# Block 6's first product by seven half-size products, with the opening's figures, the tail's stores and delays of output products

## The chip, the cores and the metric

The kernel runs on one core of a Trainium2 chip. The core has five engines with a queue each: TensorE (PE in the profile, with its weight loads as PEld), VectorE (DVE), ScalarE (ACT), GpSimd (POOL) and SyncE (SP, which here only issues transfers). They wait for one another by semaphores. PE writes to PSUM alone, eight banks of 128 partitions by 512 floats; DVE and ACT read PSUM and write to SBUF or back to PSUM. The metric is device microseconds of one execution. The time before is a median of 287.68 us over three runs (287.2 to 288.32).

## The reference

```python
scores = scale * np.matmul(q, k.transpose(0, 1, 3, 2))       # 8 batches, 8 heads, 576 positions, 64 wide
gamma = 1.0 - 2.0 ** (-5.0 - np.arange(H, dtype=np.float32))
rel = pos[:, None] - pos[None, :]
Dmat = np.where(rel >= 0, gamma[:, None, None] ** rel[None, :, :], 0.0)
attn_out = np.matmul(scores * Dmat[None, :, :, :], v)
x = np.ascontiguousarray(attn_out.transpose(0, 2, 1, 3)).reshape(B * S, H * D)    # 4608 x 512
h = x @ w_in                                                  # 4608 x 2048
g = 0.5 * h * (1.0 + erf(h / sqrt(2)))
return g @ w_out                                              # 4608 x 512
```

So an attention with a decay per head in place of a softmax comes first, and then a perceptron with a GELU between two products. Inputs and output are float32; inside, matrices are bf16 and sums are float32 in PSUM.

## The kernel before, in words

**Attention.** The 576 positions of a sequence are cut in five chunks, four of 128 and one of 64. A *unit* is one chunk of one batch (the short chunks of two batches make one unit), 36 units in all, mostly in pairs. A unit needs q and k transposed (`turn` on PE for the first groups, `turn_dma` on SP's queue for the rest), scores (`scores`, tile sc), a decay mask on DVE (`masked`, tile ret, two DVE instructions for a unit), values scaled by position (`scaled_v`, tile vh; one DVE instruction, or eight on ACT for units named in `BY_ACT`), output products (`inner`, tile o_ps), a running state of keys and values (`state`, tile u_ps), the part that comes from earlier chunks (`cross`) and the way out of PSUM into xT (`evacuate`). A pair's scores take four PSUM banks, its outputs two.

**The perceptron.** The 4608 rows are nine blocks (0 to 8) of 512, four units each. The first product of blocks 0 to 6 is plain (`mlp1`, line 683, tile hT): 64 matmuls of 512 columns for a block, or the same in smaller cuts for blocks 0 and 1, each group followed by a GELU on ACT (line 692). Blocks 7 and 8, those from `FAST` on, take it by seven half-size products instead of eight (`fast`, line 935, tile f): for each of four column groups j, the products P1 to P7 have four matmuls of 256 columns each. Their operands are sums and differences: of w_in (`sum_in`, lines 893 to 895, and `sum_last`, line 900, which overwrites a quarter of each w_in piece once the last plain block has read it) and of xT (`sum_x`, line 908). What the products give is put together in PSUM and SBUF: P1 and P7 are copied, P6 and P5 are added on DVE (lines 950 and 954), and four GELUs on ACT follow (lines 956 and 960). A group holds up to four PSUM banks.

The second product is plain for block 0 (`mlp2`, line 727, tile oT) and by seven half-size products for blocks 1 to 8 (`part`, line 855, tile m, products M1 to M7, with `after` for what DVE and ACT do behind each). Its operands are sums of g (`sum_g`, lines 757 to 761) and of w_out (`sum_w`). M6 and M7 end with the output tiles `hi` and `lo`, which `store` (line 710) sends out on SP's queue; in the last block M6's are issued from ACT's queue, and M7 comes in two halves.

**What sets the order.** The program is written out by a planner in the kernel's own source, at build time. It keeps a clock for each engine (`T`), with a cost for each operation, models the two DMA queues, and at each step writes out the piece of PE's work that is ready: attention steps first (`cand` and `due`), then perceptron pieces (`mlp_pick`). Where a first product by halves runs beside the second product of the block before, two of its products go to one of the second product (`A_TURNS`). A candidate must find free PSUM banks (`held`, `pending`, `free_time`). Conditions tie the pieces down: `AHEAD` bounds how many units attention runs ahead, `fast_ready` says when a half-size product may start. Until 16 us the planner puts filler matmuls into gaps of PE (`warm`, line 1132), behind eight fixed ones (line 1139); before the time `HOT` it takes matmuls as twice as long.

The list `ORDER` (line 325) is worked off by POOL, which issues all loads of weights (wi, wo) and of q, k and v in that order, and makes a few constants (io, dq). Its entries a... name units whose values ACT scales, and s... give a delay to a unit's scores (`S_LATE`). The first q and k are loaded by SP and ACT.

Of the kernel before, what the change touches and what calls it, by code (L numbers as in the profile page):

```python
# [17 lines left out]
def kernel(  # L18
# [51 lines left out]
    HW_FIRST = ((("q", 0),), (("k", 0),))  # L70
    FAST, ALL_FAST = 7, 7
    N_LD = 5
# [4 lines left out]
    A_TURNS = 2  # L77
    HOT = 7.5

# [240 lines left out]
    for x, keys in enumerate(zip(*HW_FIRST)):  # L320
        for n, (what, i) in enumerate(keys):
            land[what, i] = 4.75 + 1.7 * x
            t = tiles_of(i)
            cast_due[what, i] = (t[1] if what == "v" else t[0][:, "qk".index(what)], first[what, i])
    ORDER = ("wi1 k2 q1 io k1 q2 v0 v1 wi0 v2 k3 wi2 wi3 wi4 q3 wi5 wi6 v3 wi7 v4 k5 k4 q5 q4 wo1 wo0 v5 q8 wo2 "
# [3 lines left out]
             "s20+4.0 s5+3.0 s15+0.3").split()  # L329

    BY_ACT = {int(x[1:]) for x in ORDER if x[0] == "a"}
    S_LATE = {int(x[1:].split("+")[0]): float(x.split("+")[1]) for x in ORDER if x[0] == "s"}
    ORDER = [x for x in ORDER if x[0] not in "as"]

# [372 lines left out]

    def store(t, ts, src, lo=0, hi=d_model, queue=nc.sync):
        for row, p0, n in rows_of(t, ts):
            queue.dma_start(out[row:row + n, lo:hi], src[p0:p0 + n])  # L710
        for _ in rows_of(t, ts):
            hw_dma(0.4, MOVE["store"] * (hi - lo) / d_model / len(rows_of(t, ts)), max(T["act"], T["dve"]), putter(o_free, (t, ts // 2)))
# [78 lines left out]
    def after(t, p, done, half):  # L791
# [12 lines left out]
        elif p == M1:  # L804
            v = held_bank[t, "V", 0] = seeded([128, 2, 256], "m")
            for x in range(1 + last):
                xs = slice(x, x + 1) if last else slice(0, 2)
                at = either(0.42 if last else 0.68, done, v[1][:, xs], held_bank[t, "Z", x][1], -1.0)
        elif p in (M5, M2):
            at = either(0.68, max(done, o_at(t, p == M2)), lo[:, :, RIGHT] if p == M5 else hi[:, :, LEFT], m)  # L810
            release(b, at + SEM)
        elif p == M6:
            nc.vector.scalar_tensor_tensor(hi[:, :, RIGHT], m, -1.0, hi[:, :, LEFT], op0=ALU.mult, op1=MINUS)  # L813
            at = on("dve", 0.68, max(done, read_at[t, M2]))
            release(b, at + SEM)
            for x in range(2):
                if last:
                    store(t, 2 + x, hi[:, x, RIGHT], 256, 512, nc.scalar)
                else:
                    store(t, 2 + x, hi[:, x, :])  # L820
        elif last:
            nc.vector.tensor_tensor(lo[:, half, LEFT], m[:, 0], lo[:, half, RIGHT], op=MINUS)
            at = on("dve", 0.42, done)
            release(b, at + SEM)
            store(t, half, lo[:, half, LEFT], 0, 256)
        else:
            nc.vector.tensor_tensor(lo[:, :, LEFT], m, lo[:, :, RIGHT], op=MINUS)
            at = on("dve", 0.68, max(done, read_at[t, M5]))
            release(b, at + SEM)
            for x in range(2):  # L830
                store(t, x, lo[:, x, :])
# [147 lines left out]
    def fast_ready(t, j, p):  # L979
# [3 lines left out]
        if p == P1:  # L983
            if not may_begin(t, j):
                return 1e9
            if wanted[0] and lead()[0] == "3" and lead()[2] in (M3, M4, M1) or len(held) + 3 + pending() > 7:
                return 1e9
            if t >= ALL_FAST and nA < N_U and lead()[0] == "3":
                return 1e9
            if j == 2 and t < ALL_FAST and (t - 1, M1, 0) not in begun:  # L990
# [94 lines left out]
    def fire():  # L1085
# [24 lines left out]
        while later:  # L1110
            n = next((n for n, x in enumerate(later) if x[0] <= now and T[x[1]] <= now + 0.05
                      and (x[1] == "dve" or x[0] < 5.0 or all(y[3] is not make_args for y in later))), None)
# [24 lines left out]
    for _ in range(8):  # L1137
        b, t = bank([128, 512], FP32, "warm")
        nc.tensor.matmul(t, lhsT=zeros[:, :128], rhs=zeros, start=True, stop=True)  # L1139
        release(b, 0.0)  # L1140
    T["pe"] = 4.9
    while True:
# [26 lines left out]
        if nB < nA:  # L1169
# [4 lines left out]
            if any(("v", i) in cast_due for i in back):  # L1174
                ready = 1e9
            ready = max(ready, free_time(out_banks(back) + first_o))
            hurry = early or nA == N_U or stuck
# [7 lines left out]
        if g and scored < 1e8:  # L1185
            if early or stuck:
                cand(max(scored, free_time(2 * len(g))) if nA - nB <= 2 else 1e9, "S", g, [])
            else:
                late = first and (first[0] in "34" and first[1] + 1 >= FAST)
                free = head is None or late or head[1] == 0 or head[0] == "1" and (head[1] > 1 or head[4] > 0)  # L1190
                free = free or head[0] == "2" and 4 <= head[3] <= 8 or head[0] == "3"
                ahead = 4 * (first[1] - (first[0] == "4")) + AHEAD + 2 * (first[1] > 1) + 3 * bool(late) if first else 99
                if (free and all(st[i]["R"] <= now and st[i].get("V", 1e9) <= now + 0.3 for i in back)
# [3 lines left out]
                    if n + len(held) + pending() <= 8 and T["dve"] <= now + 1.0:  # L1197
                        cand(max(scored, free_time(n) - 0.3), "S", g, back)
                    elif n > 7 and n - 2 * len(g) + len(held) + pending() <= 8:
                        cand(free_time(n - 2 * len(g)) - 0.3, "S", [], back)  # L1200
# [93 lines left out]
```

## Time and profile before

| what | us |
|---|---|
| median of three runs | 287.68 |
| the profiled execution, its own time | 287.26 |
| its span, first to last instruction | 285.5 |
| PE busy, DVE busy, ACT busy | 278.0, 191.3, 151.7 |
| first scores (line 500) | 10.59 |
| first matmul of hT | 13.96 |
| second product of block 5 begins | 190.29 |
| first matmul of f (block 7) | 222.23 |
| last DVE instruction begins | 281.38 |

The page gives the busy time of each engine over the span, then groups of instructions with what ended the idle time before them. Matmuls are pipelined: the length given for one is longer than the distance from its start to the start of the next, so the distance is what a matmul costs. A table of stretches gives each engine's busy time in windows of the span, and the waits tell which engine waited for which. Between the span and the execution's own time lie 1.8 us of launch and end.

### The profile page before, as it was taken

The numbers are of one execution on the slowest core, as the hardware profiler recorded it, in microseconds if no ns is written. First come the engines' busy times: TensorE is split into PE (matmuls) and PEld (weight loads), VectorE is DVE, ScalarE is ACT, GpSimd is POOL, SyncE is SP. The second block draws the span as 40 slices with busy tenths as digits, with TensorE's granted clock in tenths as the row PEclk, the third lists the DMA queues.
The fourth block names the chain that finished last, engine by engine and source line by source line (L and its number), as shares of the span: only waits on it lengthen the run. The fifth ranks groups of instructions, "written<-read, shape, count | busy, mean of one in ns | idle before, by whom it ended". The sixth has DMA issues, their size and how long they took to land.

```text
span 285.5 us, 7980 instructions
## 1 busy us (share of the span) xinstructions
PE 278.0 (97%) x3343; PEld 204.5 (72%) x3364; DVE 191.3 (67%) x396; ACT 151.7 (53%) x339; POOL 113.8 (40%) x143
## 2 busy tenths in 40 slices
PE   7999999999999999999999999999999999999994
PEld 1699676688864588548854786468746888888883
DVE  3751693879658782998289717683598768966912
ACT  5678635565428642893255448852267454565320
POOL 8977977897156546412297454000000000000000
PEclk9999999999999999999999999999999999999999
DMA  9999999999999999999999999990210000400233
GB/s 145 164 189 170 194 183 149 214 169 152 138 162 137 193 133 152 225 125 136 158 136 174 139 152 148 228 86 3 76 73 2 0 2 0 149 0 3 76 110 111
DMA packets 152372, 35.39 MB, mean 124 GB/s; under 512 B 141072, under 2 KB 148240, under 8 KB 152336
## 3 DMA queue, kind: packets, MB, share of 16 engines
q0 software_dynamic: 116832, 18.10, 97.8%
q1 hardware_dynamic: 34160, 16.26, 32.8%
q10 hardware_dynamic: 1344, 0.52, 0.8%
q8 instruction: 26, 0.43, 0.7%
q14 instruction: 10, 0.08, 0.1%
HBM read 36.70 MB, written 9.44 MB: 162 GB/s over the span
## 4 chain that ended last, share of the span: by engine, by line
PE 93%; DVE 4%; issue 1%; ACT 0%
PE hT L683 33%; PE m L855 33%; PE f L935 9%; PE oT L727 5%; PE o_ps L584 3%; PE sc L519 3%; DVE ret L542 2%; PE qk_ps L471 2%; PE warm L1139 2%; PE u_ps L603 1%; PE o_ps L635 1%; PE warm L1132 1%; DVE xT L654 0%; PE sc L500 0%; PE sc L509 0%
## 5 line engine op out<-in xcount | busy, mean ns | idle before, releaser
L683 PE MATMUL hT<-xT,w_in 128*128 128x512 bf16 (+2 forms) x689 | 100.8, 300 | 0.8
L692 ACT ACTIVATE g<-hT 128x512 bf16<-128x512 f32 (+1 forms) x128 | 67.4, 542 | 39.9 <-PE hT L683 38.2
L683 PEld LDWEIGHTS <-w_in 128*128 128x128 bf16 x704 | 57.3, 98 | 37.2
L855 PEld LDWEIGHTS <-gs 128*128 128x128 bf16 x640 | 62.1, 98 | 8.4 <-issue 0.6
L855 PE MATMUL m<-w_sum,gs 128*128 128x256 bf16 x384 | 46.5, 273 | 0.4 <-DVE m L802 0.3
L313 POOL DMA_DIRECT2D v_ld<-in_v_dram x40 | 34.1, 865 | 18.7 <-DMA qk_ld<-in_k_dram 8.3
L542 DVE TENSOR_TENSOR ret<-sc,msk 128x512 bf16<-128x512 f32 x48 | 30.2, 682 | 15.4 <-PE sc L519 15.4
L313 POOL DMA_DIRECT2D qk_ld<-in_q_dram x36 | 30.4, 854 | 22.5 <-DMA v_ld<-in_v_dram 11.8
L313 POOL DMA_DIRECT2D qk_ld<-in_k_dram x36 | 30.3, 847 | 21.6 <-DMA qk_ld<-in_q_dram 17.1
L855 PE MATMUL m<-w_out,gs 128*128 128x256 bf16 x256 | 32.4, 273 | 0.0
L855 PE MATMUL m<-w_sum,g 128*128 128x256 bf16 x256 | 30.7, 273 | 0.0
L855 PEld LDWEIGHTS <-g 128*128 128x128 bf16 x256 | 25.0, 98 | 4.0
L757 DVE TENSOR_TENSOR gs<-g 128x1024 bf16<-128x1024 bf16 x32 | 21.7, 685 | 5.4 <-ACT g L692 5.1
L556 ACT ACTIVATE vh<-v_ld,dv 128x64 bf16<-128x64 bf16 x96 | 24.0, 339 | 0.0
L761 DVE TENSOR_TENSOR gs<-g 128x1024 bf16<-128x1024 bf16 x32 | 21.5, 682 | 0.0
L654 DVE TENSOR_TENSOR xT<-o_ps,dqT 128x512 bf16<-128x512 f32 (+1 forms) x32 | 18.4, 615 | 2.0 <-PE o_ps L635 1.9
L450 ACT COPY o<-m 128x512 f32<-128x512 f32 x14 | 8.2, 584 | 20.7 <-PE m L855 20.7
L813 DVE SCALAR_TENSOR_TENSOR o<-m,o 128x512 f32<-128x512 f32 x8 | 5.5, 690 | 20.1 <-PE m L855 15.7
L450 ACT CAST u_sb<-u_ps 128x512 bf16<-128x512 f32 x15 | 8.8, 585 | 18.2 <-PE u_ps L603 18.2
L960 ACT ACTIVATE g<-f 128x512 bf16<-128x512 f32 x24 | 13.6, 591 | 6.9 <-PE f L935 6.9
L445 DVE COPY qkT<-qk_ps 128x512 bf16<-128x512 bf16 x15 | 5.8, 420 | 16.3 <-PE qk_ps L471 16.3
L559 DVE TENSOR_TENSOR vh<-v_ld,dv 128x512 bf16<-128x512 bf16 x24 | 15.7, 680 | 0.0
(96 smaller groups left out, 307.2 us busy)
## 6 DMA issues: line engine op xcount, KB each, us to landing
out_dram<-o SPq DMA_DIRECT2D x29, 256.0 KB, 5.0
v_ld<-in_v_dram POOLq DMA_DIRECT2D x32, 128.0 KB, 9.4
qk_ld<-in_k_dram POOLq DMA_DIRECT2D x28, 128.0 KB, 8.8
qk_ld<-in_q_dram POOLq DMA_DIRECT2D x28, 128.0 KB, 10.4
w_in<-in_moe_w_in_dram POOLq DMA_DIRECT2D x8, 256.0 KB, 7.2
w_out<-in_moe_w_out_dram POOLq DMA_DIRECT2D x8, 256.0 KB, 7.9
out_dram<-o SPq DMA_DIRECT2D x11, 128.0 KB, 2.4
qk_ld<-in_k_dram POOLq DMA_DIRECT2D x8, 64.0 KB, 9.5
```

The lines of the kernel that those rows point to most:

```text
L313: nc.gpsimd.dma_start(dst, src[2 * bp + jj, :, ci * C:ci * C + n, :].rearrange("h s d -> s h d"))
L450: nc.scalar.copy(dst, src)
L542: nc.vector.tensor_tensor(r, t, by, op=ALU.mult)
L556: nc.scalar.activation(vh[:, h, :], loaded[i][1][:, h, :], AF.Copy, scale=dv[:, h, ci:ci + 1])
L559: nc.vector.tensor_tensor(vh, loaded[i][1], dv[:, :, ci:ci + 1].to_broadcast([128, H, D]), op=ALU.mult)
L654: nc.vector.tensor_tensor(x_of(i)[:, :, n * x:n * x + n], o, dqT[:, :, ci * C:ci * C + n], op=ALU.mult)
L683: nc.tensor.matmul(hT[:, m, :], lhsT=w[:, cc, o:o + 128], rhs=x_tiles[t][:, cc, lo:hi], start=(cc == 0), stop=(cc == N_DM - 1))
L692: nc.scalar.activation(g_of(t, m0 // 2)[:, m0 % 2:m0 % 2 + n, lo:hi], hT, AF.Gelu)
L757: nc.vector.tensor_tensor(s.rearrange("p m a b -> p m (a b)"), g[:, :, 0, :], g[:, :, 1, :], op=ALU.add)
L761: nc.vector.tensor_tensor(s, g[:, :, :, LEFT], g[:, :, :, RIGHT], op=MINUS)
L855: nc.tensor.matmul(m[:, 0 if apart else ts, :], lhsT=a, rhs=w, start=p in begins and mm == 0 and ts == 0, stop=mm == N_DF // 2 - 1, skip_g ...
L935: nc.tensor.matmul(m[:, y, :], lhsT=a[:, c], rhs=d[:, c], start=p in (P1, P7) and y == 0 and c == 0, stop=c == 1, skip_group_check=True)
```

## The change

`FAST` and `ALL_FAST` go from 7 to 6, so block 6 takes its first product by seven half-size products too. The rest is in the planner, in its list and in the tail:

- the list of loads, of units scaled on ACT (19 instead of 12) and of delays of scores is another, and entries b... are new: they delay a unit's output products (`B_LATE`);
- for the opening, `HOT` is 9.5 instead of 7.5, PE's clock stands at 6.33 instead of 4.9 behind the fixed fillers, the first loads land at 4.8 instead of 4.75, and leftover constants may be written when their engine is within 0.25 of PE's clock instead of 0.05;
- the condition that kept a first product by halves from starting while attention is unfinished and the second product leads is taken out;
- attention may run as far ahead beside late second products as elsewhere (`3 * bool(late)` becomes `0 * bool(late)`), and output products may be written without scores beside any second product;
- in the last block, M6's last step on DVE is made in two halves, the second half-tile first, each followed by its stores, which go to ACT's queue, SP's queue and ACT's queue.

```diff
-    FAST, ALL_FAST = 7, 7
+    FAST, ALL_FAST = 6, 6
-    HOT = 7.5
+    HOT = 9.5
...
-            land[what, i] = 4.75 + 1.7 * x
+            land[what, i] = 4.8 + 0.75 * x
...
-    ORDER = ("wi1 k2 q1 io k1 q2 v0 v1 wi0 v2 k3 wi2 wi3 wi4 q3 wi5 wi6 v3 wi7 v4 k5 k4 q5 q4 wo1 wo0 v5 q8 wo2 "
-             "wo3 dq2 wo4 wo7 a30 wo6 q6 dq3 v7 k7 wo5 v6 q7 k6 q11 q9 k10 k8 v12 v11 k9 k12 k11 q10 v10 v8 v9 q12 "
...
+    ORDER = ("k1 wi0 io v0 q1 q2 k2 v1 a35 v2 q3 k3 wi1 wi2 v3 wi3 k4 wi4 q4 wi6 wi5 q5 q6 k5 wo0 wi7 wo1 wo2 v4 "
+             "v5 dq2 wo3 wo5 k6 q8 q9 q11 q7 wo4 k7 k10 v6 wo6 v7 a15 v11 wo7 v8 a8 k11 k8 v9 q10 k9 v12 q12 dq3 "
+             "v10 k12 a7 a28 a31 a11 a32 s17+6.0 s35+1.0 s0+0.3 s29+1.5 dq4 s24+0.3 b21+2.0 a27 s8+0.3 s27+6.0 "
...
+    B_LATE = {int(x[1:].split("+")[0]): float(x.split("+")[1]) for x in ORDER if x[0] == "b"}
...
-    def store(t, ts, src, lo=0, hi=d_model, queue=nc.sync):
-        for row, p0, n in rows_of(t, ts):
+    def store(t, ts, src, lo=0, hi=d_model, *on_queues):
+        for x, (row, p0, n) in enumerate(rows_of(t, ts)):
+            queue = on_queues[x] if on_queues else nc.sync
...
-            nc.vector.scalar_tensor_tensor(hi[:, :, RIGHT], m, -1.0, hi[:, :, LEFT], op0=ALU.mult, op1=MINUS)
-            at = on("dve", 0.68, max(done, read_at[t, M2]))
+            for x in (1, 0) if last else (slice(0, 2),):
+                nc.vector.scalar_tensor_tensor(hi[:, x, RIGHT], m[:, x], -1.0, hi[:, x, LEFT], op0=ALU.mult, op1=MINUS)
+                at = on("dve", 0.42 if last else 0.68, max(done, read_at[t, M2]))
+                if last:
+                    store(t, 2 + x, hi[:, x, RIGHT], 256, 512, nc.scalar, nc.sync)
...
-            if t >= ALL_FAST and nA < N_U and lead()[0] == "3":
-                return 1e9
...
-            n = next((n for n, x in enumerate(later) if x[0] <= now and T[x[1]] <= now + 0.05
+            n = next((n for n, x in enumerate(later) if x[0] <= now and T[x[1]] <= now + 0.25
...
-    T["pe"] = 4.9
+    T["pe"] = 6.33
...
-            ready = max(ready, free_time(out_banks(back) + first_o))
+            ready = max(ready + B_LATE.get(back[0], 0.0), free_time(out_banks(back) + first_o))
...
-                ahead = 4 * (first[1] - (first[0] == "4")) + AHEAD + 2 * (first[1] > 1) + 3 * bool(late) if first else 99
+                ahead = 4 * (first[1] - (first[0] == "4")) + AHEAD + 2 * (first[1] > 1) + 0 * bool(late) if first else 99
...
-                    elif n > 7 and n - 2 * len(g) + len(held) + pending() <= 8:
+                    elif (n > 7 or first[0] == "3") and back and n - 2 * len(g) + len(held) + pending() <= 8:
```

More of the change, by code (lines that the diff above doesn't have):

```diff
@@ L321 @@
         for n, (what, i) in enumerate(keys):
-            land[what, i] = 4.75 + 1.7 * x
+            land[what, i] = 4.8 + 0.75 * x
             t = tiles_of(i)
             cast_due[what, i] = (t[1] if what == "v" else t[0][:, "qk".index(what)], first[what, i])
-    ORDER = ("wi1 k2 q1 io k1 q2 v0 v1 wi0 v2 k3 wi2 wi3 wi4 q3 wi5 wi6 v3 wi7 v4 k5 k4 q5 q4 wo1 wo0 v5 q8 wo2 "
[3 rows of a table removed]
-             "s20+4.0 s5+3.0 s15+0.3").split()
+    ORDER = ("k1 wi0 io v0 q1 q2 k2 v1 a35 v2 q3 k3 wi1 wi2 v3 wi3 k4 wi4 q4 wi6 wi5 q5 q6 k5 wo0 wi7 wo1 wo2 v4 "
[4 rows of a table added]
+             "b22+0.3 b23+0.3 s28+1.5 a22 a26 s20+1.0 a30 s18+1.0").split()
     BY_ACT = {int(x[1:]) for x in ORDER if x[0] == "a"}
     S_LATE = {int(x[1:].split("+")[0]): float(x.split("+")[1]) for x in ORDER if x[0] == "s"}
-    ORDER = [x for x in ORDER if x[0] not in "as"]
+    B_LATE = {int(x[1:].split("+")[0]): float(x.split("+")[1]) for x in ORDER if x[0] == "b"}
+    ORDER = [x for x in ORDER if x[0] not in "abs"]
     rest = const.tile([128, 2], BF16, name="rest")
@@ L812, in after @@
         elif p == M6:
-            nc.vector.scalar_tensor_tensor(hi[:, :, RIGHT], m, -1.0, hi[:, :, LEFT], op0=ALU.mult, op1=MINUS)
-            at = on("dve", 0.68, max(done, read_at[t, M2]))
-            release(b, at + SEM)
[L816 to L820, printed above, removed]
+            for x in (1, 0) if last else (slice(0, 2),):
[3 more added lines that the diff above has]
+                    store(t, 2 + x, hi[:, x, RIGHT], 256, 512, nc.scalar, nc.sync)
+            release(b, at + SEM)
+            for x in range(2 * (not last)):
+                store(t, 2 + x, hi[:, x, :])
         elif last:
```

4 rows, old and new, of the table ORDER are left out of this document.

## The prediction

> **What bounds the kernel now.** I read the page's shares first, then what ended the waits of TensorE (PE), then a table of stretches cut where the work changes kind, then the timeline at both ends.
>
> ```profile
> PE 278.0 (97%) x3343; PEld 204.5 (72%) x3364; DVE 191.3 (67%) x396; ACT 151.7 (53%) x339; POOL 113.8 (40%) x143
> ```
>
> All waits of PE (us in total, times, longest):
>
> ```profile
> PE warm L1139 <- DVE zeros L116: 1.2, 1, 1.2
> PE m L855 <- DVE m L802: 0.3, 1, 0.3
> PE oT L727 <- issue: 0.2, 1, 0.2
> ```
>
> One real stall, 0.3 us. So the end is set by when PE first has steady work, by the sum of its matmuls, and by what follows the last one. The stretches (columns: busy time and count of PE, its weight loads, DVE, ACT, POOL; clock, DMA share, GB/s):
>
> ```profile
> 0.00:15.42 15.42, 13.67 (x107) 6.43 (x109) 9.23 (x38) 9.38 (x22) 14.32 (x23) 1.00 1.64 157
> ...
> 222.39:264.75 42.36, 42.36 (x391) 37.97 (x389) 31.16 (x54) 22.92 (x42) 0.00 (x0) 1.00 0.08 26
> 264.75:281.38 16.63, 16.59 (x152) 14.62 (x150) 8.09 (x15) 3.34 (x7) 0.00 (x0) 1.00 0.28 97
> ```
>
> The first is the opening, where busy includes filler matmuls. In the second, blocks 7 and 8 run their first product as seven half-size ones (f) between the second product of the block before (m): PE is busy for all of 42.36 us, with DVE at 74%. The stage that the change rebuilds, second product of block 5 and first of block 6, is this one:
>
> ```profile
> 190.07:219.83 29.76, 29.60 (x350) 20.04 (x352) 20.83 (x43) 14.77 (x31) 0.00 (x0) 1.00 0.11 38
> ```
>
> Two timelines, of PE in the opening and of the last pieces:
>
> ```profile
> 7.57 1.06 PE L471 MATMUL qk_ps<-ident,qk 128*128 128x128 bf16 x8
> ...
> 10.59 0.40 PE L500 MATMUL sc<-qkT 64*128 64x128 bf16 x8
> ```
> ```profile
> 279.69 0.69 DVE L813 SCALAR_TENSOR_TENSOR o<-m,o 128x512 f32<-128x512 f32 x1 [3.23 <-PE m L855]
> 280.41 1.62 ACTq L710 DMA_DIRECT2D out_dram<-o  x3
> 280.51 0.42 DVE L822 TENSOR_TENSOR o<-m,o 128x256 f32<-128x256 f32 x1
> 281.38 0.42 DVE L822 TENSOR_TENSOR o<-m,o 128x256 f32<-128x256 f32 x1 [0.45 <-PE m L855]
> ```
>
> **Block 6 by seven products.** Out go 64 matmuls of 512 columns, which start 216 ns apart in the hT rows; in come 4 groups x 7 products x 4 = 112 of 256 columns, 109 ns apart in the f rows (a group's mean of 379 or 273 ns is one matmul's length in the pipe, not its share). 64 x 0.216 = 13.82; 112 x 0.109 = 12.21: **-1.62 us** of PE. The 48 more weight loads, 98 ns each, are hidden: in 222.39:264.75 37.97 us of loads lie inside 42.36 us of gapless matmuls. [...]
>
> DVE pays. Each of four groups needs two adds (L950, L954: 0.69 each, 5.5 us in all) and two copies that go to DVE (0.69) or ACT (0.58); in blocks 7 and 8 nine of 16 were DVE's, so 3.1 us more. Four sums of x (L908) at 0.42 are 1.7, which block 7 already paid in this stage and now pays later. The in-place weight differences (L900, 8 x 0.28) move from 211-221 to before 190, where DVE is busy 11.28 of 16.7 us; without that idle time they cost 2.2. The other weight sums (L893 to L895) end by 135.0 already. GELU on ACT costs the same 9.6 (16 x 0.60, or 4 x (0.63 + 3 x 0.59)). Six of them lay in this stage (1.7). So DVE asks 20.83 + 5.5 + 3.1 - 1.7 = 27.7 us of a stage that shrinks to 29.76 - 1.62 = 28.1: 99%, unless work leaves it.
>
> Work does leave. The list sends the scaled values of 19 units, not 12, to ACT: -7 x 0.68 = -4.8 on DVE, +7 x 2.0 = 14 on ACT (L556 takes 24.0 for 96), over the whole run, two or so in this stage. ACT, at 14.77 of 29.76, hides it; if not, a GELU queued behind one such unit waits 2.0 and with it a PSUM bank. The rest can go later: block 8 first needs its units at about 243, while their last xT came at 220. The guard that kept half-size products from starting while attention is unfinished is gone, so its last groups now run among them, and the eight PSUM banks are shared three ways: a pair of units asks six, a group of half-size products holds up to four, the second product two to four. That is the new wait: scores stand behind a draining group, and PE has only m to run meanwhile. Ends: 0 as in 222.39:264.75, and +5 for one group's length (42.36 / 8 = 5.3) lost once. The delays of output products (12 units) and of scores choose where; so do the dropped allowance of three units ahead beside late second products, and the leave to run output products without scores beside any second product. I take **+0.4**, near the 0.3 of the one stall that m has with attention beside it, since the two pairs can be put where m runs alone.
>
> **The opening.** Planner figures change, and the order of POOL's loads with them. Landings now: 128-row loads 0.9 apart, w_in pieces 1.33 apart; k1 at 9.22, v0 11.08, q2 10.18, second w_in piece 12.80. In the new order (k1 wi0, constants, v0 q1 q2 k2 v1 v2 q3 k3 wi1 ...) the same steps give v0 at 8.5, q1 9.4, v1 12.1, and the three fillers at 6.34 (1.44 us) are no longer placed, since the planner holds PE busy until 6.33 and not 4.9. First scores come at about 8 instead of 10.6, first hT at 11 instead of 13.96. Against that, w_in is late: wi1 about 16.1 and the last piece 30.9, where now all eight are there by 25. PE has its block 0 first product (256 x 56 ns = 14.3) complete at 32.7 rather than 31.6, and fills in with the second product, whose weights come earlier (29.6 against 30.6, then two more by 33.8). Counting matmuls in both orders up to 47 us, the new one has done 16 of 256 columns more (1.74), less one oT (0.22) and eight transposes (0.45), 0.5 us later: **-0.6**. Ends: -2.9 (all of the earlier scores kept) and +2.3 (1.1 later w_in plus 1.2 of holes between pieces, with nothing filled). POOL's count of loads and their 0.85 each don't change; the constants left over may start 0.2 earlier beside PE's clock (0.25 for 0.05), which shifts ACT and DVE instructions of under 0.5 and lies within these ends. The clock belongs here: fillers start 0.64 apart at first and 0.22 apart from 9.6 on. [...] This trace shows only the release near 9.5.
>
> **The tail.** The last M6 step becomes two DVE passes of 0.42 for one of 0.69, with stores on ACT, SP and ACT in place of three on ACT. The last store hangs on the last M7 half (281.38 + 0.42), is issued at 281.83 on SP and lands at 283.94; the third on ACT lands at 283.60. SP's M2 stores are issued by 279.99, so the added one fits before 280.96. The first M7 half slips by 0.1 and still ends 0.4 before the last. **0**, ends -0.1 and +0.3 (one more SP issue ahead of the last).
>
> Instruction fetch: 96 more PE instructions on 6707; no wait of PE shows one, so 0.
>
> **Sum.** -1.62 + 0.4 - 0.6 + 0 = -1.8. The profiled execution took 287.26 (span 285.5 and 1.8 around it), which gives 285.4; it was 0.42 under the median of 287.68, so 285.9 for the median.
>
> **The rivals.** (1) The stage at 190 to 218 stalls, on banks or on DVE. For it: 99% of DVE on paper, and six banks for a pair. Against: 74% in 222 to 265, and 25 us of slack for block 8's units. One whole group drained costs 5.3, so -1.8 - 0.4 + 5.3 = +3.1: 290.8. It decides from 2.2 us of stalls on (no gain), 3.6 for slower. (2) w_in comes too late and PE has holes between 16 and 40, the fillers missing: -1.62 + 0.4 + 2.3 = +1.1, 288.8. For it: 20 to 30 us is a stretch with DMA at full share. Against: the fill-in counted above. (3) The change doesn't do what it says: PE's saved time turns into waits for units still loading. Last transposed keys land at 191.8, 50 us before block 8 needs them, so small: 287.3.
>
> **How the numbers follow.** 0.5% (1.4 us) is about what a measurement tells from no change. Forecast 0.55, all of it faster. Rival 1 0.25: small stalls (within 0.5%) 0.11, large 0.14. Rival 2 0.15, half each way: 0.08 and 0.07. Rival 3 0.05, same. Faster 0.55, same 0.24, slower 0.21. The forecast's own range is 284.3 to 286.3, by an opening between -2.0 and 0. The whole range goes from 284.3 to 289.8, leaving about 0.1 beneath and 0.1 above, for a drained group.
>
> **What would show it.** Right: f matmuls 336 instead of 224, hT 640, f beginning near 190; last matmul near 279.5; in the second stage PE busy all the time; first scores near 8. Wrong: PE waiting for DVE f or p, or sc and o_ps behind f, between 190 and 220; gaps between w_in pieces at 16 to 32; a last store that is not M7's.

## The result, and the profile after

| | us |
|---|---|
| before, median of 22 runs | 287.76 (286.62 to 288.38) |
| after, median of 22 runs | 289.52 (287.16 to 292.36) |
| after : before | 1.0049, 95% interval 1.0028 to 1.0070 |
| forecast | 285.9 |

The change makes the kernel slower by about half a per cent. Medians and extremes here hold every execution, while the ratios leave out those that took over 1.5% longer than the fastest of their kernel, five of the changed kernel's 22. The times after spread more than those before, and the profiled execution, at 291.9 us (span 290.0), is one of the long ones. In nine of the 22 the mean granted clock was 0.992 to 0.994 and the time 290.6 to 292.4; in the other 13 it was 0.997 to 1.0 and the time 287.2 to 290.2, with a median of 288.67. So about 0.9 us of the loss stands in executions whose clock was whole.

The page's shares, and all waits of PE (us in total, times, longest):

```profile
PE 281.7 (97%) x3411; PEld 209.8 (72%) x3411; DVE 204.2 (70%) x417; ACT 161.5 (56%) x388; POOL 114.1 (39%) x143
```
```profile
PE sc L521 <- DMA qkT<-qk_ld: 1.9, 1, 1.9
PE warm L1140 <- DVE zeros L116: 1.2, 1, 1.2
PE qk_ps L473 <- DMA qk<-in_q_dram: 0.5, 1, 0.5
PE m L858 <- issue: 0.2, 1, 0.2
```

Before had no wait over 0.3 us behind the start. Now there is one of 1.9: scores (sc) for transposed keys (qkT). The stretches, cut as before (PE, weight loads, DVE, ACT, POOL, clock, DMA share, GB/s), of the opening, the rebuilt stage (second product of block 5 and first of block 6) and what follows it:

```profile
0.00:15.42 15.42, 13.30 (x88) 5.81 (x88) 8.60 (x38) 8.79 (x20) 14.30 (x23) 1.00 1.68 154
...
196.00:225.00 29.00, 29.00 (x335) 24.35 (x332) 25.06 (x44) 15.12 (x32) 0.00 (x0) 1.00 0.05 19
225.00:266.00 41.00, 41.00 (x378) 36.75 (x376) 32.79 (x59) 19.05 (x35) 0.00 (x0) 1.00 0.12 41
```

The rebuilt stage has no hole: PE is busy for all of 29.00 us and DVE for 86%. The loss stands elsewhere. The timeline of PE around the one long wait:

```profile
118.68 0.38 PE L685 MATMUL hT<-xT,w_in 128*128 128x512 bf16 x1
118.99 0.64 PE L586 MATMUL o_ps<-ret,v_ld 128*64 128x128 bf16 x16
119.46 0.42 PE L605 MATMUL u_ps<-vh,qk_ld 128*64 128x64 bf16 x16
121.83 0.64 PE L521 MATMUL sc<-qkT 64*64 64x128 bf16 x32 [1.95 <-DMA qkT<-qk_ld]
122.40 4.88 PE L685 MATMUL hT<-xT,w_in 128*128 128x512 bf16 x14
```

These are the scores of units 20 and 21. The next table cuts that place in three: the wait, the 3.4 us behind it, and the 3.4 us after those.

```profile
119.50:121.80 2.30, 0.38 (x22) 0.27 (x16) 0.14 (x1) 1.76 (x4) 0.71 (x1) 1.00 1.44 100
122.50:125.93 3.43, 3.43 (x9) 1.19 (x9) 3.43 (x6) 0.60 (x1) 2.25 (x3) 0.50 1.45 288
126.00:129.40 3.40, 3.40 (x17) 1.57 (x16) 2.70 (x7) 2.34 (x4) 0.24 (x1) 1.00 1.64 154
```

Behind the wait the clock is 0.50 for 3.43 us: 9 matmuls start where 17 do later. So in this execution the wait costs its 1.95 us, and about 1.7 more (half of 3.41).

Last, the tail: the stores on SP's and ACT's queues, M6's two passes (L817) and M7's halves (L825):

```profile
279.91 7.16 SPq L713 DMA_DIRECT2D out_dram<-o  x8
...
284.60 0.76 DVE L817 SCALAR_TENSOR_TENSOR o<-m,o 128x256 f32<-128x256 f32 x2 [3.23 <-PE m L858]
285.05 1.38 ACTq L713 DMA_DIRECT2D out_dram<-o  x2
285.41 0.42 DVE L825 TENSOR_TENSOR o<-m,o 128x256 f32<-128x256 f32 x1
286.29 0.42 DVE L825 TENSOR_TENSOR o<-m,o 128x256 f32<-128x256 f32 x1 [0.45 <-PE m L858]
```

From the start of PE's last matmul to the end of the span it took 4.41 us before and 4.02 here.

**Where the 4.5 us between the two spans lie.** I count PE's work: every matmul issued by some moment, each at its gapless distance (0.216 for 512 columns, 0.109 for 256, 0.056 for 128, the small ones of attention at their means). What the changed kernel has done less than before by the same moment is its *lag*. The trace of before lacks 20 records of matmuls of 512 columns, which are counted in. A lag is read at single moments between matmuls, so each figure is good to about 0.2 us.

| up to | lag of after | what it gained there |
|---|---|---|
| 48 us | 1.30 | opening |
| 112 us | 1.53 | 0.2 |
| 136 us | 5.61 | 4.1: the wait and the half clock |
| 192 us | 5.64 | 0 |
| 232 us | 6.50 | 0.9: the rebuilt stage |
| 280 us | 6.50 | 0 |

Its whole work is 1.59 us less (263.13 against 264.72), and the tail is 0.4 shorter: 6.50 - 1.59 - 0.39 = 4.5.

### The profile page after: what moved, and what is told of

Its sections match the earlier page's. It is cut to its first block, busy times and chain, and to the rows that moved or that the text cites. A ratio compares the mean times of both kernels' runs of the same rounds, so it can differ in the third digit from the quotient of the medians.

```text
span 290.0 us, 8186 instructions
## 1 busy us (share of the span) xinstructions
PE 281.7 (97%) x3411; PEld 209.8 (72%) x3411; DVE 204.2 (70%) x417; ACT 161.5 (56%) x388; POOL 114.1 (39%) x143
## 4 chain that ended last, share of the span: by engine, by line
PE 79%; DMA 15%; POOL 4%; issue 1%; DVE 0%; POOLq 0%; SPq 0%
PE m L858 30%; PE hT L685 23%; PE f L938 13%; PE oT L730 5%; DMA qk_ld<-in_k_dram 4%; DMA qk_ld<-in_q_dram 4%; DMA qkT<-qk_ld 4%; DMA w_in<-in_moe_w_in_dram 3%; PE o_ps L586 2%; PE sc L521 2%; POOL qk L313 2%; PE o_ps L637 1%; POOL v_ld L313 1%; PE u_ps L605 1%; PE qk_ps L473 1%; POOL w_in L286 1%
## 5 line engine op out<-in xcount | busy, mean ns | idle before, releaser
L685 PE MATMUL hT<-xT,w_in 128*128 128x128 bf16 (+2 forms) x640 | 89.1, 297 | 0.1
L694 ACT ACTIVATE g<-hT 128x512 bf16<-128x512 f32 (+1 forms) x112 | 58.5, 534 | 33.7 <-PE hT L685 31.5
L685 PEld LDWEIGHTS <-w_in 128*128 128x128 bf16 x640 | 52.0, 98 | 32.9 <-issue 2.4
L858 PE MATMUL m<-w_sum,gs 128*128 128x256 bf16 x384 | 48.3, 273 | 0.3 <-issue 0.2
L558 ACT ACTIVATE vh<-v_ld,dv 128x64 bf16<-128x64 bf16 x152 | 37.6, 337 | 1.3 <-DMA v_ld<-in_v_dram 1.3
L858 PE MATMUL m<-w_out,gs 128*128 128x256 bf16 x256 | 33.4, 273 | 0.0
L963 ACT ACTIVATE g<-f 128x512 bf16<-128x512 f32 x36 | 20.6, 590 | 11.6 <-PE f L938 9.2
L938 PEld LDWEIGHTS <-w_in 128*128 128x128 bf16 x192 | 18.8, 98 | 2.3
L959 ACT ACTIVATE g<-p 128x512 bf16<-128x512 f32 x12 | 7.6, 630 | 18.8 <-DVE p L957 18.8
L447 DVE COPY qkT<-qk_ps 128x512 bf16<-128x512 bf16 x17 | 6.6, 420 | 13.1 <-PE qk_ps L473 12.6
L938 PEld LDWEIGHTS <-wi 128*128 128x128 bf16 x144 | 14.1, 98 | 1.8 <-issue 0.2
```

Of the source, the lines that this page charges most:

```text
L558: nc.scalar.activation(vh[:, h, :], loaded[i][1][:, h, :], AF.Copy, scale=dv[:, h, ci:ci + 1])
L685: nc.tensor.matmul(hT[:, m, :], lhsT=w[:, cc, o:o + 128], rhs=x_tiles[t][:, cc, lo:hi], start=(cc == 0), stop=(cc == N_DM - 1))
L694: nc.scalar.activation(g_of(t, m0 // 2)[:, m0 % 2:m0 % 2 + n, lo:hi], hT, AF.Gelu)
L858: nc.tensor.matmul(m[:, 0 if apart else ts, :], lhsT=a, rhs=w, start=p in begins and mm == 0 and ts == 0, stop=mm == N_DF // 2 - 1, skip_g ...
L938: nc.tensor.matmul(m[:, y, :], lhsT=a[:, c], rhs=d[:, c], start=p in (P1, P7) and y == 0 and c == 0, stop=c == 1, skip_group_check=True)
L963: nc.scalar.activation(g[:, :, rows, cols], m, AF.Gelu)
```

## The experiments

Theory 1 was that scores now stand close behind the transfers of their keys, so that PE waits, and a wait takes the clock down. Theory 2 was that the opening makes the loss. All kernels below compute everything. Ratios are against before, measured beside them on the same chip.

**1. The wait at units 20 and 21 taken away.** The scores of these units are due 5.0 us behind their keys and not 1.0; the rest of the plan stays.

```diff
-             ... s28+1.5 a22 a26 s20+1.0 a30 s18+1.0").split()
+             ... s28+1.5 a22 a26 s20+5.0 a30 s18+1.0").split()
```

> The changed kernel with one figure of its list altered: the scores of units 20 and 21 are due 5.0 us after their keys instead of 1.0, so the planner writes out about 20 more matmuls of block 3's first product ahead of them; the rest of the program keeps its order. Theory 1 (PE stands still at 120 us because these keys land at 121.8, and then runs at half speed): the wait of 1.9 us and the half speed behind it (about 1.9 us) go, the granted clock is 1.000, the span falls from 290.0 to about 286, and the time is near that of the kernel before, 287.0 to 288.0. Rival (the loss lies in the opening and in block 6's stage, and the wait would only move): another wait of 1 to 2 us takes its place and the time stays near 289.

Measured: 288.08 (286.67 to 291.52, 12 runs), ratio 1.0006 (0.9986 to 1.0026). PE in the profile around the same place:

```profile
123.32 0.64 PE L586 MATMUL o_ps<-ret,v_ld 128*64 128x128 bf16 x16
123.79 0.42 PE L605 MATMUL u_ps<-vh,qk_ld 128*64 128x64 bf16 x16
124.14 0.64 PE L521 MATMUL sc<-qkT 64*64 64x128 bf16 x32
124.71 2.55 PE L685 MATMUL hT<-xT,w_in 128*128 128x512 bf16 x10
```

No wait, and the clock stays (mean of the execution 1.0). In this execution the keys had landed at 117.8; in the changed kernel's at 121.8, at the same place of the program. So here the keys were early as well as the scores late. The span is 286.3, against 290.0. The lag at 48 us is still 1.5 to 1.7, so theory 2 is not touched by it.

**2. The wait filled.** Ten matmuls of zeros ahead of the same scores, so that PE is not idle while it waits.

```diff
     def scores(n):
         g = groups[n]
+        if n == 13:
+            b, t = bank([128, 512], FP32, "warm")
+            for _ in range(10):
+                nc.tensor.matmul(t, lhsT=zeros[:, :128], rhs=zeros, start=True, stop=True)
+            release(b, T["pe"])
```

> The changed kernel with ten filler matmuls (2.16 us) right ahead of the scores of units 20 and 21; the wait for their keys is not shortened, PE only works through it. If the half speed behind the wait comes from PE's standing still, it goes: hT behind these scores starts 0.216 apart instead of 0.43, the granted clock is 1.000, the span is about 288.1. If the half speed has another cause, it stays and the span is 290. If the wait is not what costs time, the fillers add 2.2 us: 292.

Measured: 290.34 (289.49 to 291.93, 4 runs), ratio 1.0090 (1.0056 to 1.0124). It was a poor test: in the profiled execution the keys landed at 118.0, there was nothing to fill, and the fillers were 2.2 us of added work. So it does not say whether the half clock comes from PE's standing still. One came in the opening of this execution (11.10 to 14.51), behind a wait of 1.6 us for the second q.

**3. Block 6 plain again, all the rest as changed.**

```diff
-    FAST, ALL_FAST = 6, 6
+    FAST, ALL_FAST = 7, 7
```

> The changed kernel with block 6's first product plain again (both block figures 7), and all else as changed, the wait at 120 us too. Theory 1 (the seven products do what they are for, 1.62 us less two marking matmuls of 0.22): about 1.2 us slower than the changed kernel, 290.5 on the mean of its runs. Rival (the stage of block 6 costs what it saves or more): same or faster than the changed kernel, 288 to 289.5.

Measured: 290.06 (288.36 to 293.23, 10 runs), ratio 1.0075 (1.0047 to 1.0104). So the loss comes without the seven products: it lies in the rest of the change. The products themselves win about 0.7 us here (1.0049 with them, 1.0075 without), though the two intervals overlap. The same wait is there, with keys landing at 122.5:

```profile
119.83 0.42 PE L605 MATMUL u_ps<-vh,qk_ld 128*64 128x64 bf16 x16
122.59 0.64 PE L521 MATMUL sc<-qkT 64*64 64x128 bf16 x32 [2.34 <-DMA qkT<-qk_ld]
```

**4. The other way: block 6 by products, with the three conditions it needs, on before's own list, opening and tail.**

```diff
-    FAST, ALL_FAST = 7, 7
+    FAST, ALL_FAST = 6, 6
...
-            if t >= ALL_FAST and nA < N_U and lead()[0] == "3":
-                return 1e9
...
-                ahead = ... + 3 * bool(late) if first else 99
+                ahead = ... + 0 * bool(late) if first else 99
...
-                    elif n > 7 and n - 2 * len(g) + len(held) + pending() <= 8:
+                    elif (n > 7 or first[0] == "3") and back and n - 2 * len(g) + len(held) + pending() <= 8:
```

> The kernel before with block 6 by seven products and the conditions that go with it (no guard, no allowance of three units, output products without scores), but with its own list, opening and tail. If the products alone carry the gain: 1.62 less some marking matmuls, 286.4 to 286.9. If the list's delays and units for ACT are needed for them (rival 1 of the prediction: banks and DVE in the stage of 190 to 220): waits of PE appear there and the time is 288.5 to 290.

Measured: 289.13 (288.04 to 290.71, 10 runs), ratio 1.0048 (1.0024 to 1.0072). A miss: on before's list the products and their conditions lose as much as the whole change does. The longest waits of PE:

```profile
PE sc L519 <- DMA qkT<-qk_ld: 2.0, 2, 1.8
PE warm L1137 <- DVE zeros L116: 1.2, 1, 1.2
PE oT L727 <- DMA w_out<-in_moe_w_out_dram: 0.7, 1, 0.7
```

The long one is for units 29 and 30, at 169.29. The stage behind 190 is without a hole here too (PE 30.00 of 30.00 us). The opening is not behind (0.45 us ahead at 25). Attention has moved up against its loads: the scores of units 29 and 30 stood at 175.9 in before and are ready for PE at 167.5 here, and a wait of nearly 2 us for keys is the price at yet another place.

**5. The tail alone, on the kernel before** (the parts of the diff in `store` and `after`).

```diff
-            nc.vector.scalar_tensor_tensor(hi[:, :, RIGHT], m, -1.0, hi[:, :, LEFT], op0=ALU.mult, op1=MINUS)
-            at = on("dve", 0.68, max(done, read_at[t, M2]))
...
+            for x in (1, 0) if last else (slice(0, 2),):
+                nc.vector.scalar_tensor_tensor(hi[:, x, RIGHT], m[:, x], -1.0, hi[:, x, LEFT], op0=ALU.mult, op1=MINUS)
...
+                    store(t, 2 + x, hi[:, x, RIGHT], 256, 512, nc.scalar, nc.sync)
```

> The kernel before with the change's tail alone: M6 of the last block in two halves, its stores on the queues of ACT, SP and ACT. The prediction's term was 0. From the two traces, 4.41 us from the last matmul to the end became 4.02, since the last store landed 1.73 us after its issue instead of 2.11: 0.4 us faster, 287.4, if this comes from the third ACT store being out of the way; 287.8 if it is chance.

Measured: 287.41 (286.43 to 289.78, 12 runs), ratio 0.9988 (0.9965 to 1.0012). In the profile the tail is 0.38 us shorter (4.03 against 4.41); the interval of the times holds that and also nothing.

**6. The opening's figures alone, on the kernel before.**

```diff
-    HOT = 7.5
+    HOT = 9.5
...
-            land[what, i] = 4.75 + 1.7 * x
+            land[what, i] = 4.8 + 0.75 * x
...
-            n = next((n for n, x in enumerate(later) if x[0] <= now and T[x[1]] <= now + 0.05
+            n = next((n for n, x in enumerate(later) if x[0] <= now and T[x[1]] <= now + 0.25
...
-    T["pe"] = 4.9
+    T["pe"] = 6.33
```

> The kernel before with the change's opening figures alone (PE's clock 6.33 behind the fillers, matmuls taken as twice as long until 9.5, first loads at 4.8, constants within 0.25), its list as before. [...] Rival (the figures are nearer to the trace, so the opening gains): 0.5 us faster, 287.2.

Measured: 287.75 (286.82 to 289.82, 10 runs), ratio 1.0010 (0.9978 to 1.0042). The forecast gain of 0.5 us did not come. The profiled execution lags by 0.9 to 1.0 us from the opening on, yet the median shows nothing. When the full clock was granted does not explain this lag: that was at 9.49 here and at 9.51 in before. What the figures do show is in the clocks of the single executions: in two of the ten the mean was 0.994 and 0.993, and these took 289.4 and 289.8 us. In 139 executions of before, measured beside the experiments, no clock was under 0.996.

**7 and 8. Sixteen gapless fillers at the start** (in one bank, not eight in a bank each), on the kernel of experiment 1 and on before, to have the clock granted early: it came at 13.24 us in the one and at 9.51 in the other. If the late grant sets the opening back, PE's work at 25 us comes level with before's.

```diff
-    for _ in range(8):
-        b, t = bank([128, 512], FP32, "warm")
+    b, t = bank([128, 512], FP32, "warm")
+    for _ in range(16):
```

> The changed kernel with the later scores of units 20 and 21 as in the first experiment, and the eight opening fillers, which start 0.64 apart in eight banks, replaced by sixteen in one bank with no gaps between them. [...] Rival (the opening is behind because the pieces of w_in are loaded later): the work done by 25 us stays 1.0 to 1.5 us behind and the time stays at 288.0.

> The kernel before with sixteen gapless opening fillers in one bank instead of eight. If the clock is what counts, it is released by 8 us instead of 9.5 and the start is 0.3 to 0.6 us ahead: 287.2. If only the loads set the opening: 287.7. If the sixteen run at half speed to 8 us and stand in front of the first transposes: 288.3.

Measured: 289.31 (288.08 to 291.36, 12 runs), ratio 1.0061 (1.0039 to 1.0083), and on before 287.59 (12 runs), 1.0001 (0.9982 to 1.0020). On the changed kernel the fillers did harm. The full clock came at 4.21 us instead, and PE then waited:

```profile
7.92 0.39 PE L1133 MATMUL warm<-zeros 128*128 128x512 bf16 x1
9.81 0.62 PE L473 MATMUL qk_ps<-ident,qk 128*128 128x128 bf16 x8 [1.50 <-DMA qk<-in_q_dram]
10.78 0.40 PE L473 MATMUL qk_ps<-ident,qk 128*128 128x128 bf16 x4 [0.35 <-DMA qk<-in_q_dram]
```

and from 11.04 to 14.46 the clock was half again; the lag at 25 us was still 1.4 to 1.5. So an early grant does not by itself mend the opening: in this execution the early waits for q, and the half clock behind them, have taken the place of the late grant.

**9. A wider distance planned for all later units.** The change's list without the b entries, with the scores of all units from 18 on due at least 5.0 us behind their keys' planned time.

```diff
-                g, scored = groups[n], sg[n]["T"] + S_LATE.get(nA, 0.0)
+                g, scored = groups[n], sg[n]["T"] + max(S_LATE.get(nA, 0.0), 5.0 if nA >= 18 else 0.0)
```

> The changed kernel with the scores of all units from 18 on due at least 5.0 us behind the planned time of their keys (the change leaves 2.3 to 9.6 us there), and without the b entries, which alter nothing in the order of PE. Theory 1 (scores stand close behind their keys' transfers): what the run with 5.0 us at units 20 and 21 alone gave, 288.1, or up to 0.4 less where other keys came late too: 287.6 to 288.3; no wait of PE for qkT over 0.5 us behind 100 us. Theory 2 (the opening costs the rest): the kernel is still 1.2 us of PE work behind before at 25 us, so that it does not come under 287.2. If the wait at units 20 and 21 was an accident of one execution, this is 289.5 like the changed kernel.

Measured: 289.23 (288.21 to 294.92, 12 runs), ratio 1.0040 (1.0018 to 1.0062). A miss: no better than the change by its interval. The wait was gone at units 20 and 21 (scores at 126.10, keys at 119.5) and came back at units 31 and 32, whose keys landed as late as 181.9:

```profile
181.97 0.64 PE L520 MATMUL sc<-qkT 64*64 64x128 bf16 x32 [1.19 <-DMA qkT<-qk_ld]
```

A planned distance is no distance when the transfers themselves run late.

**10 and 11. Before's order of loads and its choice of units scaled on ACT**, in the changed kernel, with the 5.0 us of experiment 9 and without, again without the b entries. The diff is the list:

```diff
-    ORDER = ("k1 wi0 io v0 q1 q2 k2 v1 a35 v2 q3 k3 wi1 wi2 v3 wi3 k4 wi4 q4 wi6 wi5 q5 q6 k5 wo0 wi7 wo1 wo2 v4 "
...
+    ORDER = ("wi1 k2 q1 io k1 q2 v0 v1 wi0 v2 k3 wi2 wi3 wi4 q3 wi5 wi6 v3 wi7 v4 k5 k4 q5 q4 wo1 wo0 v5 q8 wo2 wo3 dq2 "
+             "wo4 wo7 wo6 q6 dq3 v7 k7 wo5 v6 q7 k6 q11 q9 k10 k8 v12 v11 k9 k12 k11 q10 v10 v8 v9 q12 dq4 a30 a8 a28 "
```

> The same margin of 5.0 us, with the list of loads and the units scaled on ACT of before; the change's delays of scores, its opening figures, half-size products in block 6 and its tail stay. If keys and opening together made the loss: 1.59 us less for block 6, 0.5 more for marking matmuls and mode changes, 0 to 0.4 less for the tail, and an opening within 0.3 of before's: 286.0 to 287.2 against 287.7. If the opening figures (not the order of the loads) set the opening back: another 0.9 to 1.2 more, 287.2 to 288.2. If neither theory holds, 289 or above.

> As the run before it, without the margin of 5.0 us. Theory 1: the plan puts scores again 2 to 6 us behind the keys of their units, whose landings were up to 6 us later than planned, so PE waits once or twice for qkT between 100 and 190 us, 1 to 2.5 us in all, and the run is 0.7 to 2.5 us above the one with the margin. If the margins don't matter with this order of loads: the same within 0.4.

Measured: 287.96 (286.90 to 290.43), ratio 1.0014 (0.9988 to 1.0040) with, and 287.86 (286.58 to 290.83), 0.9997 (0.9970 to 1.0024) without; 12 runs each. The planned distance, which theory 1 had put in the centre, made no difference. With this order the loss was gone either way, and no profile of the two has a wait for qkT. Theory 1 had to be restated: not how near the plan puts scores to keys, but how late this order of loads makes the keys. Nor was anything won, though the openings are level (lag 0.0 to 0.3 at 48 us). In the two profiles the lag is 0.9 and 1.6 us at 192 and 1.5 and 2.3 us at 232, which uses up the 1.6 of block 6's products and the 0.4 of the tail.

**12. The order of the loads alone.** The list's loads and constants (57 entries, not 72 as the forecast has it) go back to before's order, nothing else.

> The changed kernel with one thing undone: the 72 loads and constants in its list go back to before's order. The change's units scaled on ACT, its delays of scores and of output products, its opening figures, block 6 by products and its tail stay. If the order of the loads alone made the loss: 287.4 to 288.3, PE within 0.3 us of before's work at 48 us, no wait for qkT over 1 us. If the units scaled on ACT or the delays made it: 289 to 290. If a short distance from keys to scores (the plan has 2 to 3 us at units 17 to 21 here) makes it whatever the order of loads: 288.3 to 289.5 with a wait for qkT of 1 to 2 us between 95 and 190 us.

Measured: 287.61 (286.46 to 289.02, 12 runs), ratio 0.9992 (0.9972 to 1.0011). One part of the change undone takes away the loss. The keys of units 20 and 21 landed at 117.8, their scores ran at 118.66 without a wait, and PE had no wait over 0.6 us but the first. The lag at 48 us, 0.88, was not within the 0.3 expected.

**13 to 15. Which loads?** The first 18 entries of before's list with the change's order behind them; the change's first 18 with before's order behind them; and the change's list with a single load moved, k12, from its end to in front of k8:

```diff
-   ... v11 wo7 v8 k11 k8 v9 q10 k9 v12 q12 dq3 v10 k12 ...
+   ... v11 wo7 v8 k11 k12 k8 v9 q10 k9 v12 q12 dq3 v10 ...
```

> The changed kernel with the first 18 loads of its list as before has them (wi1 k2 q1 io k1 q2 v0 v1 wi0 v2 k3 wi2 wi3 wi4 q3 wi5 wi6 v3); the other 39 in the change's order, k12 last. If the loss stands in the opening: 287.4 to 288.2, and PE at 48 us ahead of the changed kernel by 0.5 us or more. If it stands in the later loads (k12 last, so that the transposes of units 11 and 12 and all behind them start late): the transposed keys of units 20 and 21 land at 119 to 122, PE waits 1 to 2 us for them in most executions, 289 to 290.

> The other way round: the first 18 loads as the change has them, the other 39 in before's order. If the loss stands in the later loads: 287.5 to 288.4, keys of units 20 and 21 landed by 118.5. If it stands in the opening: 288.8 to 290.

> The changed kernel with one load moved: k12, the last of its list, goes seven places ahead, in front of k8. If k12's landing (64.1 us in the changed kernel, 54 to 56 where before's order of loads stands) is what holds the transposes of units 11 and 12 back, the keys of units 11 and 12 land by 75.5 instead of 77.2, those of 20 and 21 by 118.5, and the time is 287.6 to 288.6. If the chain of transposes is held by something else, its landings stay and the time is 289 to 290.

| kernel, 12 runs each | median | ratio (95%) | keys of units 11, 12 landed | of 20, 21 |
|---|---|---|---|---|
| after (22 runs) | 289.52 | 1.0049 (1.0028 to 1.0070) | 77.2 | 121.8 |
| first 18 as before | 288.88 | 1.0051 (1.0019 to 1.0082) | 76.4 | 117.6 |
| the rest as before | 287.98 | 1.0018 (0.9996 to 1.0040) | 73.9 | 117.0 |
| k12 alone moved | 287.89 | 1.0009 (0.9989 to 1.0028) | 74.6 | 116.6 |

The landings are those of one profiled execution each. The later loads make the loss: with before's order there it is gone within the interval, and before's first 18 do not help. Moving one load takes most of it away, 0.4% or 1.2 us by the ratios (1.0049 and 1.0009), though the two intervals just touch (1.0028). The queue of SP, which issues the transposes, shows the way from one to the other. After, and then with k12 moved (start, us, what is issued):

```profile
61.40 15.90 SPq L484 DMA_TRANSPOSE qkT<-qk_ld  x4
...
82.89 7.13 SPq L484 DMA_TRANSPOSE qkT<-qk_ld  x2
...
91.33 22.86 SPq L484 DMA_TRANSPOSE qkT<-qk_ld  x6
```
```profile
61.04 13.51 SPq L484 DMA_TRANSPOSE qkT<-qk_ld  x4
...
82.27 4.55 SPq L484 DMA_TRANSPOSE qkT<-qk_ld  x2
...
89.59 20.96 SPq L484 DMA_TRANSPOSE qkT<-qk_ld  x6
```

Each transpose waits in this queue for its operand (in the changed kernel SP waited 20.4 us for loads of q and 7.4 for loads of k), and the queue issues them in the order of the units. In the changed kernel k12 is issued at 55.5 and lands at 64.1, last of its group, so the transpose of unit 12 can't start until 64.3 and its keys land at 77.2; with k12 moved it lands at 54.0, and q12, now last, at 58.9, the transpose starts at 63.4 and lands at 74.6. The first row, units 11 to 14, ends 2.8 us sooner, and the loads of later units, which take the buffers that transposes set free (at 148.67 in the changed kernel, after 7.34 us of waiting for one), follow: q20 is issued at 87.8 instead of 93.7. How 0.9 us at the start grows to that on the way is not broken down, and it need not: in experiment 1, with the change's order and k12 landed at 63.0, q20 was issued at 88.7. The seven profiles with k12 last fit this. In four of them (after, experiments 3, 7 and 9) k12 landed at 63.9 to 64.8, and the keys of units 20 and 21 at 119.5 to 122.5. In three (experiments 1, 2 and 13) it landed at 60.5 to 63.0, and those keys at 117.6 to 118.0. In nine of the ten profiles with k12 earlier in the list the keys landed at 116.0 to 117.8; in the tenth, experiment 4, at 119.4. In the profile with k12 moved the scores of units 20 and 21 run without a wait, 2.4 us behind their keys:

```profile
118.23 0.64 PE L586 MATMUL o_ps<-ret,v_ld 128*64 128x128 bf16 x16
118.70 0.42 PE L605 MATMUL u_ps<-vh,qk_ld 128*64 128x64 bf16 x16
119.04 0.64 PE L521 MATMUL sc<-qkT 64*64 64x128 bf16 x32
119.62 7.73 PE L685 MATMUL hT<-xT,w_in 128*128 128x512 bf16 x34
```

What is argued and not shown: that the wait occurs in the other long runs of the changed kernel too (each kernel has one trace). The profile with before's first 18 has no wait for qkT either, with 1.4 us to spare, though its ratio is the change's. Keys landed up to 5 us apart in the seven kernels with this order (117.6 in experiment 13, 122.5 in experiment 3), so a distance of 1 to 3 us may hold in some executions and not in others.

Nor is it shown where the half clock lay in the other eight runs of the changed kernel with a low mean, and there is a rival for it: the opening. Experiments 2 and 7 have their half clock there (11.10 to 14.51 and 11.04 to 14.46), behind waits for q of 1.6 us and of 1.50 and 0.35. Over all executions, a mean clock under 0.9955 occurred only in kernels with the change's opening figures: in 38 of 154, against none of 173 in those without them (before, experiments 4, 5 and 8). Late keys alone, as in experiment 4, brought none in ten. So some of the long executions may owe their half clock to the opening, and the order of the loads then accounts for the rest.

No kernel here is shown to beat the one before; the best ratios, 0.9988 and 0.9992, have intervals that hold 1.

## Why the prediction was wrong

**Block 6 by seven products, -1.62: right.** f has 336 matmuls, 109 to 110 ns apart, hT 640, and PE's work is 1.59 us less. The weight loads stayed hidden: 332 of them, 24.35 us, lie inside 29.00 us of PE without a hole. Only its place is off: f begins at 199.9, and at 195.4 with k12 moved, not near 190.

**The stage, +0.4: right in kind, measured 0.7 to 0.9.** No stall, so the first rival fell: DVE came to 25.06 of 29.00 us, not 99%. In two undisturbed profiles of the same span, 285.5 (before, and k12 moved), the lag grows by about 0.8 us from 192 to 232. Two marking matmuls (of zeros, which prepare a PSUM bank for f) at 0.216 us are half of that. A change from perceptron to attention lengthens a distance from 0.109 to 0.20 us; there are 36 in the program instead of 32, but only one of the four more lies in this stage. The rest is not broken down.

**The tail, 0: a little better,** -0.4 in most profiles, outside the ends given (-0.1 to +0.3). From PE's last matmul to the end it is 4.00 to 4.05 us in eleven of the 13 profiles with the new tail, against 4.38 to 4.41 in the four without; in two (experiments 2 and 7) it is 4.44, and why is not known. The last store is M7's, as said, and lands 1.73 us after its issue instead of 2.11. The times alone do not resolve it.

**The opening, -0.6: mis-sized, with the wrong sign.** First scores came at 8.13, as said; first hT at 13.77, not 11. The lag at 48 us is 1.30 us in the profile of the changed kernel and 0.4 to 1.7 in those with the change's opening figures and units scaled on ACT, whatever the order of loads. When the full clock is granted is a part of it at most: that was at 13.29 us here against 9.51 before, but with the first 18 loads as before it was at 7.64, and the lag at 48 us still 1.2; there one wait of 1.1 us for a q at 25 us made most of it. With before's loads and before's units scaled on ACT together (experiments 10 and 11) the lag at 48 us is 0.0 to 0.3. The second rival, holes for late w_in pieces, fell as it was put: no wait of hT for w_in is among the rows of the changed kernel, and with k12 moved such waits come to 0.7 us, where the rival had 1.2 of holes. How much of the lag each part of the list makes stays open.

**The steps that failed** are two. One is a term of the sum: the opening's -0.6 came out as +0.9 to +1.3, which by itself takes most or all of the forecast gain of 1.8 away. The other made a loss of it. It is the sentence under the third rival, "Last transposed keys land at 191.8, 50 us before block 8 needs them, so small". The mechanism was named and looked for at the wrong units: the sentence weighs the last keys against block 8, and the new list's landings were followed only to 47 us, where k12, its last load, had not yet landed. The trace of before had the number: the keys of units 20 and 21 landed at 117.2, and their scores stand 3.6 us behind them, without a wait:

```profile
120.76 0.64 PE L519 MATMUL sc<-qkT 64*64 64x128 bf16 x32
```

A list whose last load is one of the group that all later transposes queue behind had to be followed through to there. In the profiled execution the wait and the half clock cost 4.1 us, and the place of k12 costs about 1.2 us by the ratios. It is not the only way to such a wait: in experiment 4 before's order of loads stands, and the products and their conditions alone brought one.

With the keys in time the terms come out as follows, as the profile with k12 moved has them against before: -1.6 for block 6, +0.9 for the opening, +0.4 between 48 and 192 us, for which the forecast had no term, +0.8 for the stage, -0.4 for the tail. Together that is +0.1 to within the 0.2 of each, and both spans are 285.5. The gain of the products was real; it went to the opening and to the stretches where attention and perceptron alternate, and the late keys made it a loss. (A slip on the side: an opening between -2.0 and 0 gives the range 284.5 to 286.5 by the forecast's own sum, and 0.2 less was written.)

## What to carry to other kernels

When a list of loads is reordered, take the last landing of each group, follow it through every queue and buffer behind it, and set it against the first use of every group, not only in the opening. Hold the distance against the spread of landings between executions (here up to 5 us), for which one trace is not enough. A short idle time of PE in the middle of dense work may cost more than its length: in the profiled execution a wait of 1.95 us, with 3.41 us at half clock behind it, cost 4.1. And where the mean clock of single executions is on record, compare how often it is low in each kernel: in the three profiles with a mean under 0.9955 the half clock stood behind a wait of PE, so a low mean may point at waits that no kept trace has.

## What the runs showed of the hardware

In one execution TensorE's clock was halved behind a wait of under 2 us. In the changed kernel the full clock was granted at 13.29 us and withdrawn at 122.52, for 3.41 us; PE had stood still from 119.88 to 121.83, 1.95 us. The half clocks of experiments 2 and 7 lasted 3.41 and 3.42 us (11.10 to 14.51, 11.04 to 14.46), behind a wait of 1.6 us in the one and of 1.50 and 0.35 in the other. Not every such wait brought one: in experiment 3 a wait of 2.34 us left the clock at 1.00, and so did one of 1.76 us in experiment 4 (the mean of both executions is 1.0). So a wait of 2 us can cost 2 or nearly 4, and what decides between them is not shown here.

The delays of output products did nothing: built without the b entries, the changed kernel is the same program.
